# Trailing the feed-forward blocks by four slots instead of two, gathering by column halves, and moving two copies from VectorE to GpSimd

## The chip, the cores and the metric

The kernel runs on one core of one Trainium2 chip. The metric is device time in microseconds (us) of one execution; lower is better. The engines are TensorE (PE, with its weight loads PEld), VectorE (DVE), ScalarE (ACT), GpSimd (POOL) and SyncE (SP, which only issues transfers here).

## The reference

Eight batches of eight heads of causal sliding-window attention with a linear position bias (576 rows, head size 64, window 128), whose output, rows by heads, goes through two matrix products with an ELU between them.

```
scores = scale * np.matmul(q, k.transpose(0, 1, 3, 2))
bias = slopes[:, None, None] * (-np.abs(rel))[None, :, :]
mask = (rel >= 0) & (rel < 128)
attn = softmax(np.where(mask, scores + bias[None], -1e9))
x = np.matmul(attn, v).transpose(0, 2, 1, 3).reshape(B * S, H * D)    # 4608 x 512
h = x @ w_in                                                          # 512 x 2048
g = np.where(h > 0.0, h, np.exp(np.minimum(h, 0.0)) - 1.0)
out = g @ w_out                                                       # 2048 x 512
```

## The kernel before

The whole program is one list of slots, written out by hand. In each slot every engine gets its instructions in the order of the source, and it works them off in that order; there is no scheduler behind it.

**Attention.** Batch b has the sixteen slots from `s0 = 16 b` on. Slot s of it is one call of `scores` (a bank of 512 scores: four matmuls or eight half ones), with the exponential on ScalarE behind it. From batch 1 on the mask is applied by `cut`, a minimum on VectorE over two SBUF operands. One slot later comes `values` (the product with v), in some slots `normalize` (a reciprocal and a product on VectorE), and one slot after that `turn`, which lays 128 rows of the normalised output as columns into `xT`. For batches 0 and 1 `turn` is four PE transposes and a VectorE copy, from batch 2 on a transposing transfer on SP's queue (L424).

**Feed-forward (MoE in the names).** The 4608 rows are cut into nine blocks of 512, each with sixteen calls of `hidden` and sixteen of `output`, one of each per slot. `hidden` is 8 or 16 matmuls into a PSUM bank `hp` (two buffers), then an exponential on ScalarE into `e`, then a clamp of `e` on GpSimd (L457). `elu` on VectorE (L464), one slot later, joins `e` and `hp` into `g` and so frees the `hp` bank. `output` is four matmuls of 512 columns (L493); every fourth one is copied out by ScalarE and stored by SP. The tables `HID` and `OUT` name the slots. Block t begins with `hidden` in slot 4 + 16 t, and from block 2 on two slots later, because its rows are ready only then; so slots 36 and 37 have no `hidden`, and slots 45 and 46 no `output`. In a slot PE does `hidden`, then `values` of the slot before, then `scores`, then `output`. VectorE does `elu` of the slot before first.

**q, k and v of later batches.** GpSimd's queue loads them from HBM (`load_qk`, `load_tail`, `load_v4`, `load_v4_tail`); issuing such a load takes time on GpSimd itself. For batches 2 to 7 q and k are turned to head-size-by-rows form in two steps: `squares` (eight VectorE stream transposes of 32 x 32 squares into the one buffer `tt`, L318) and `collect` (eight SBUF-to-SBUF transfers on SP's queue from `tt` into `QK`, L324). `QK[b % 2]` and `VP[b % 2]` hold q, k and v of a batch. Each of the four row blocks i of `QK` is waited for by its own first `scores`. v is laid into `VP` by four small copies per row block n: `place_v4` does so on VectorE (batches 0 to 2), `place_by_pool` on GpSimd (batches 3 to 7). The constant rows 64 to 127 of `QK[1]`, among them what `fill_k` writes, are made in slots 10 to 14 and copied to `QK[0]` once by a transfer in slot 20 (`fill_other`).

Of the kernel before, what the change touches and what calls it, by code (L numbers as in the profile page):

```python
# [12 lines left out]
ALU = mybir.AluOpType  # L13
# [6 lines left out]
def kernel(  # L20
# [9 lines left out]
    nc = tc.nc  # L30
    B, H, S, D = q.shape
# [4 lines left out]
    NTB = NTOK // 512  # L36
    MID = S // 2
    XBAR = 2
    RING = 3 * S
    VW = D + 2  # L40
    V = nc.vector

# [10 lines left out]
    def one(shape, dt, name):  # L53
        return const.tile(shape, dt, name=name, tag=name)
# [12 lines left out]
    QK = [one([128, 2, 5, H, 128], F16, f"QK{i}") for i in range(2)]  # L67
    VP = [one([128, 5, H, VW], F16, f"VP{i}") for i in range(2)]
    EX = [one([128, 576], F16, f"EX{i}") for i in range(4)]
    w_in_sb = one([128, 4, FF], F16, "wi")  # L70
    w_out_sb = one([128, NFC, DO], F16, "wo")
    xT = one([128, 4, RING], F16, "xT")

# [63 lines left out]
    with tc.manual_schedule():  # L137
# [76 lines left out]
        g_, r_ = slice(64, 96), slice(96, 128)  # L214
# [3 lines left out]
        TK = one([128, 640], F16, "TK")  # L218
# [37 lines left out]
                           TQ[64:128, 128 * n:128 * n + 128].unsqueeze(1).broadcast_to([64, H, 128]))  # L256

        def fill_k(n):
            V.tensor_copy(QK[1][g_, 1, n, :, :],
                          TK[g_, 128 * n:128 * n + 128].unsqueeze(1).broadcast_to([32, H, 128]))  # L260

        def k_term(h):
            V.tensor_scalar(out=QK[1][r_, 1, :, h, :], in0=TK[r_, :].rearrange("p (n c) -> p n c", c=128),
# [49 lines left out]
        def squares(b, n):  # L313

            if b not in tt:
                tt[b] = stage.tile([128, 2, 2, H, 4, 32], F16, name="tt", tag="tt", bufs=1)
            w, dh, hs = 1 - n // 4, n // 2 % 2, slice(4 * (n % 2), 4 * (n % 2) + 4)
            V.transpose(out=tt[b][:, w, dh, hs, :, :].rearrange("p h j i -> p (h j) i"),  # L318
                        in_=stq[b][:, w, hs, :, 32 * dh:32 * dh + 32].rearrange("p h j d -> p (h j) d"))

        def collect(b, n):

            i, dh = n // 2, n % 2
            nc.sync.dma_start(  # L324
                QK[b % 2][32 * dh:32 * dh + 32, :, i, :, :].rearrange("p w h c -> p w (h c)"),
                tt[b][32 * i:32 * i + 32, :, dh, :, :, :].rearrange("p w h j i -> p w (h j i)"))
# [92 lines left out]
        def turn(b, i):  # L419
            n = 128 if i < 4 else 64  # L420
            if b >= XBAR:
                x = xnt.pop((b, i)).rearrange("p h d -> p (h d)")
                o = (b * S + 128 * i) % RING
                nc.sync.dma_start_transpose(out=xT[:, :, o:o + n], in_=x[0:n, :])  # L424
# [3 lines left out]
            for c in range(4):  # L428
                nc.tensor.transpose(t[:, c, :], x[:, c, :], ident)
            o = (b * S + 128 * i) % RING  # L430
            V.tensor_copy(xT[:, :, o:o + n], t[:, :, 0:n])
# [11 lines left out]
        def hidden(t, j):  # L443
            w, c0, f0, nf = place(t, j)
            p = hps[t, j] = ps_h.tile([128, 512], F32, name="hp", tag="hp")
            a = (512 * t + c0) % RING
            cuts = [(0, w, a)] if a + w <= RING else [(0, RING - a, a), (RING - a, w, 0)]
            for l in range(nf):
                fc = f0 + l
                for u0, u1, x0 in cuts:  # L450
                    for c in range(4):
                        nc.tensor.matmul(  # L452
                            p[:, l * w + u0:l * w + u1], w_in_sb[:, c, fc * 128:(fc + 1) * 128],
                            xT[:, c, x0:x0 + u1 - u0], start=(c == 0), stop=(c == 3))
            e = es[t, j] = work.tile([128, 512], F32, name="e", tag="e")
            nc.scalar.activation(e, p, AF.Exp)  # L456
            nc.gpsimd.tensor_scalar(out=e, in0=e, scalar1=1.0, scalar2=0.0, op0=ALU.min, op1=ALU.max)  # L457

        def elu(t, j):
            w, c0, f0, nf = place(t, j)  # L460
            if t not in gs:
                gs[t] = gpool.tile([128, NFC, 512], F16, name="g")
            sh = lambda ap: ap.rearrange("p (l c) -> p l c", c=w)
            V.scalar_tensor_tensor(  # L464
                out=gs[t][:, f0:f0 + nf, c0:c0 + w], in0=sh(es.pop((t, j))), scalar=1.0,
                in1=sh(hps.pop((t, j))), op0=ALU.subtract, op1=ALU.max)
# [36 lines left out]
        def warm(n):  # L503

            for _ in range(n):
                nc.tensor.matmul(spare[:, 0:128], ident, ident, start=True, stop=True)  # L506
# [4 lines left out]
        def at(s, f, *a):  # L511
            tasks.setdefault(s, []).append((f, a))


        HID = {4 + m + (2 if m >= 32 else 0): divmod(m, 16) for m in range(16 * NTB)}
        OUT, O0 = {}, 13
        for t in range(NTB):
            for j in range(16):
                OUT[O0 + 16 * t + j + (2 if t > 1 else 0)] = (t, j)
        warm(34)  # L520
        transposes_half(0, 0)
        transposes_half(0, 1)
# [5 lines left out]
        for b in range(B):  # L528
            s0 = 16 * b
            for s in range(16):  # L530
                i, p = BANKS[s]
                half = p if i in (0, 4) else p // 2
                at(s0 + s, scores, b, s)
                if b:
                    at(s0 + s, cut, b, s)
                at(s0 + s + 1, values, b, s)
                if i in (0, 4) or p % 2:
                    at(s0 + s + 1, normalize, b, i, half)
                    if half:
                        at(s0 + s + 2, turn, b, i)  # L540
            if b == 0:
                at(5, transposes_half, 1, 0)
                at(6, transposes_half, 1, 1)
                at(12, transposes_tail, 0)
            if b + 1 < B:
                for hp in range(NP if b == 0 else 0):
                    at((14, 14, 15, 15)[hp], transposes, 1, hp)
                for n in range(8 if b else 0):
                    at(s0 + (n if b > 1 else 6 + n // 2), squares, b + 1, n)
                    at(s0 + (8 if b > 1 else 10) + n // 2, collect, b + 1, n)  # L550
                at(s0 + (14 if b else 25), transposes_tail, b + 1)
            if b + 2 < B and b:
                at(s0 + 14, load_v4, b + 2)
                at(s0 + 19, load_v4_tail, b + 2)
                for n in range(4):
                    for u in range(2):
                        at(s0 + 20 + 2 * n + u, place_by_pool, b + 2, n, u)
                for i, w in enumerate((1, 0)):
                    at(s0 + 10 + 2 * i, load_qk, b + 2, w)
                    at(s0 + 11 + 2 * i, load_tail, b + 2, w)  # L560
# [10 lines left out]
        for n in range(5):  # L571
            at(10 + n, fill_q, n)
            at(10 + n, fill_k, n)
# [13 lines left out]
        at(11, load_v4, 1)  # L587
        at(14, load_v4_tail, 1)
        at(18, load_v4, 2)
        at(33, load_v4_tail, 2)  # L590
        for n in range(4):
            at(15 + n, place_v4, 1, n)
            at(32 + n, place_v4, 2, n)

        for s in range(max(OUT) + 1):
            if s in HID:
                hidden(*HID[s])
            if s - 1 in HID:
                elu(*HID[s - 1])
            for f, a in tasks.get(s, []):  # L600
# [33 lines left out]
```

## Time and profile before

| what | value |
|---|---|
| three runs, median (lowest to highest) | 372.12 us (369.16 to 373.36) |
| the profiled execution, its own time | 368.4 us |
| its span, first to last instruction | 366.6 us |
| mean granted clock of TensorE, share of full speed | 0.975 |
| busy share of the span: PE, DVE, ACT, POOL | 92%, 71%, 52%, 51% |

The profiled execution is below the fastest of the three runs. 1.8 us of its time lie outside the span. The rows below are from its trace; L numbers are lines of the kernel before.

### The profile page before, as it was taken

The numbers are of one execution on the slowest core, as the hardware profiler recorded it, in microseconds if no ns is written. First come the engines' busy times: TensorE is split into PE (matmuls) and PEld (weight loads), VectorE is DVE, ScalarE is ACT, GpSimd is POOL, SyncE is SP. The second block draws the span as 40 slices with busy tenths as digits, with TensorE's granted clock in tenths as the row PEclk, the third lists the DMA queues.
The fourth block names the chain that finished last, engine by engine and source line by source line (L and its number), as shares of the span: only waits on it lengthen the run. The fifth ranks groups of instructions, "written<-read, shape, count | busy, mean of one in ns | idle before, by whom it ended". The sixth has DMA issues, their size and how long they took to land.

```text
span 366.6 us, 9293 instructions
## 1 busy us (share of the span) xinstructions
PE 335.6 (92%) x3598; PEld 243.9 (67%) x3598; DVE 261.4 (71%) x604; ACT 189.2 (52%) x330; POOL 186.4 (51%) x291
## 2 busy tenths in 40 slices
PE   7879888999767989995999999999999999999994
PEld 6768765767544767774777677767767777766651
DVE  6479998797797769963888598768977766633430
ACT  3464874555333655562565456555565566443431
POOL 9144524435342882884368927883883223233320
PEclk9996999999996999998999999999999999999999
DMA  8999958969921599369935993699363142212112
GB/s 114 201 205 107 170 57 134 196 104 147 194 35 31 115 161 146 59 146 150 122 60 130 141 171 56 142 158 151 66 143 76 37 60 44 52 36 52 30 45 70
DMA packets 67435, 39.53 MB, mean 108 GB/s; under 512 B 30976, under 2 KB 59648, under 8 KB 67328
## 3 DMA queue, kind: packets, MB, share of 16 engines
q0 software_dynamic: 41904, 18.35, 43.7%
q1 hardware_dynamic: 25488, 20.59, 27.8%
q8 instruction: 28, 0.46, 0.6%
q14 instruction: 15, 0.12, 0.1%
HBM read 36.70 MB, written 9.44 MB: 126 GB/s over the span
## 4 chain that ended last, share of the span: by engine, by line
PE 54%; DVE 15%; POOL 14%; DMA 6%; issue 4%; ACT 3%; SPq 1%; ACTq 0%; POOLq 0%; DVEq 0%
PE hp L452 23%; PE op L493 20%; POOL VP L122 7%; PE sp L349 5%; POOL e L457 5%; DMA QK<-tt 4%; DVE VP L117 4%; DVE g L464 3%; PE av L395 3%; DVE tt L318 2%; DMA stq<-in_q_dram 1%; DVE xn L416 1%; DVE EX L381 1%; ACT EX L373 1%; POOL stq L81 1%
## 5 line engine op out<-in xcount | busy, mean ns | idle before, releaser
L457 POOL TENSOR_SCALAR e<-e 128x512 f32<-128x512 f32 x144 | 88.9, 617 | 159.1 <-ACT e L456 155.8
L452 PE MATMUL hp<-xT,wi 128*128 128x256 f16 (+3 forms) x1536 | 153.2, 249 | 13.7 <-DVE g L464 8.6
L452 PEld LDWEIGHTS <-wi 128*128 128x128 f16 x1536 | 123.7, 99 | 56.4 <-issue 12.4
L456 ACT ACTIVATE e<-hp 128x512 f32<-128x512 f32 x144 | 86.0, 597 | 132.7 <-PE hp L452 124.0
L493 PE MATMUL op<-wo,g 128*128 128x512 f16 x576 | 148.2, 383 | 0.0
L464 DVE SCALAR_TENSOR_TENSOR g<-e,hp 128x512 f16<-128x512 f32 x144 | 96.8, 672 | 34.6 <-POOL e L457 33.8
L373 ACT ACTIVATE EX<-sp 128x512 f16<-128x512 f32 x128 | 75.9, 593 | 18.8 <-PE sp L369 10.2
L381 DVE TENSOR_TENSOR EX<-EX,band 128x512 f16<-128x512 f16 x112 | 53.2, 475 | 35.0 <-ACT EX L373 34.7
L493 PEld LDWEIGHTS <-g 128*128 128x128 f16 x576 | 51.6, 99 | 37.5 <-issue 1.1
L122 POOL TENSOR_SCALAR VP<-vs 32x512 f16<-32x512 f16 x80 | 51.4, 643 | 5.5
L349 PE MATMUL sp<-QK 128*128 128x128 f16 (+3 forms) x576 | 50.6, 216 | 0.4 <-DVE QK L297 0.4
L395 PE MATMUL av<-VP,EX 128*128 128x65 f16 x576 | 39.3, 195 | 8.1 <-DVE EX L381 3.8
L395 PEld LDWEIGHTS <-EX 128*128 128x128 f16 x576 | 31.3, 99 | 14.3 <-DVE EX L381 6.6
L416 DVE TENSOR_TENSOR xn<-av,rden 128x256 f16<-128x256 f32 x80 | 33.9, 424 | 2.8
L318 DVE STREAM_TRANSPOSE tt<-stq 128x512 f16<-128x512 f16 x48 | 33.2, 697 | 1.3 <-DMA QK<-tt 1.3
L349 PEld LDWEIGHTS <-QK 128*128 128x128 f16 (+1 forms) x576 | 31.8, 98 | 1.4 <-DVE QK L297 0.5
L497 ACT COPY ob<-op 128x512 f32<-128x512 f32 x36 | 21.1, 586 | 14.8 <-PE op L493 6.5
L415 DVE RECIPROCAL rden<-av 128x4 f32<-128x4 f32 x80 | 13.9, 174 | 13.9 <-PE av L395 13.4
L117 DVE COPY VP<-vs 32x512 f16<-32x512 f16 x48 | 17.0, 354 | 1.0 <-DMA vs<-in_v_dram 0.3
L506 PE MATMUL spare<-ident 128*128 128x128 f16 x94 | 9.0, 273 | 1.6 <-DVE ident L163 1.6
L506 PEld LDWEIGHTS <-ident 128*128 128x128 f16 x94 | 8.1, 128 | 1.7 <-DVE ident L163 1.6
L297 ACT COPY QK<-tp 64x1024 f16<-64x1024 f16 x6 | 6.0, 1008 | 6.2 <-PE tp L288 4.8
(71 smaller groups left out, 124.1 us busy)
## 6 DMA issues: line engine op xcount, KB each, us to landing
out_dram<-ob SPq DMA_DIRECT2D x128, 64.0 KB, 1.7
QK<-tt SPq DMA_DIRECT2D x48, 128.0 KB, 2.5
stq<-in_k_dram POOLq DMA_DIRECT2D x7, 512.0 KB, 8.4
stq<-in_q_dram POOLq DMA_DIRECT2D x7, 512.0 KB, 8.4
vs<-in_v_dram POOLq DMA_DIRECT2D x7, 512.0 KB, 9.8
wi<-in_moe_w_in_dram POOLq DMA_DIRECT2D x4, 512.0 KB, 11.3
wo<-in_moe_w_out_dram POOLq DMA_DIRECT2D x4, 512.0 KB, 12.8
QK<-QK SPq DMA_DIRECT2D x1, 1280.0 KB, 12.9
```

The costliest lines, as they stand in the source:

```text
L122: nc.gpsimd.tensor_scalar(out=VP[b % 2][32 * j:32 * j + 32, n, :, 0:D], in0=vs[b][32 * n:32 * n + 32, :, j, :], scalar1=1.0, scalar2=0.0, ...
L318: V.transpose(out=tt[b][:, w, dh, hs, :, :].rearrange("p h j i -> p (h j) i"), in_=stq[b][:, w, hs, :, 32 * dh:32 * dh + 32].rearrange("p ...
L349: nc.tensor.matmul(t[:, o:o + n], qk[0:r, 1, kc, h, :], qk[0:r, 0, qc, h, 0:n], start=b > 0 or o == 0, stop=b > 0)
L373: nc.scalar.activation(e[:, 0:512], t, AF.Exp, scale=0.125)
L381: V.tensor_tensor(out=e, in0=e, in1=band[:, c:c + n].unsqueeze(1).broadcast_to([128, 512 // n, n]), op=ALU.min)
L395: nc.tensor.matmul(a[:, l, :], e[:, c:c + 128], vp[:, n, h, 0:D + 1], start=st, stop=sp)
L416: V.tensor_tensor(out=xnt[b, i][:, 4 * half:4 * half + 4, :], in0=a[:, :, 0:D], in1=r.unsqueeze(2).broadcast_to([128, 4, D]), op=ALU.mult)
L452: nc.tensor.matmul(p[:, l * w + u0:l * w + u1], w_in_sb[:, c, fc * 128:(fc + 1) * 128], xT[:, c, x0:x0 + u1 - u0], start=(c == 0), stop=(c ...
L456: nc.scalar.activation(e, p, AF.Exp)
L457: nc.gpsimd.tensor_scalar(out=e, in0=e, scalar1=1.0, scalar2=0.0, op0=ALU.min, op1=ALU.max)
L464: V.scalar_tensor_tensor(out=gs[t][:, f0:f0 + nf, c0:c0 + w], in0=sh(es.pop((t, j))), scalar=1.0, in1=sh(hps.pop((t, j))), op0=ALU.subtrac ...
L493: nc.tensor.matmul(ops[t], gs[t][:, fc, ts * 128:(ts + 1) * 128], w_out_sb[:, fc, :], start=(fc == 0), stop=(fc == NFC - 1))
```

## The change

It edits five places.

1. `HID` and `OUT`: from block 2 on, `hidden` and `output` come four slots later than for blocks 0 and 1, not two. So slots 36 to 39 have no `hidden`, slots 45 to 48 no `output`, and the program has two slots more behind the attention.
2. `squares` goes through its eight pieces by halves of the head size (`dh`) first, and for batches 3 to 7 begins two slots later (third slot of the batch before, not first).
3. `collect` goes through the four row blocks of one half, then those of the other. One goes out per slot, in slots 8 to 15 (batch 2) or 6 to 13 (batches 3 to 7) of the batch before, where two per slot went out in slots 10 to 13 or 8 to 11.
4. v of batch 2 is placed by GpSimd (16 instructions, slots 24 to 31) and not by VectorE (16 instructions, slots 32 to 35); its tail is loaded in slot 22, not 33.
5. `fill_k` (five instructions, slots 10 to 14) is on GpSimd, not VectorE.

```diff
+    LATER = 4
         def fill_k(n):
-            V.tensor_copy(QK[1][g_, 1, n, :, :],
-                          TK[g_, 128 * n:128 * n + 128].unsqueeze(1).broadcast_to([32, H, 128]))
+            nc.gpsimd.tensor_scalar(
+                out=QK[1][g_, 1, n, :, :], in0=TK[g_, 128 * n:128 * n + 128].unsqueeze(1)
+                .broadcast_to([32, H, 128]), scalar1=1.0, scalar2=0.0, op0=ALU.mult, op1=ALU.add)
...
-            w, dh, hs = 1 - n // 4, n // 2 % 2, slice(4 * (n % 2), 4 * (n % 2) + 4)
+            dh, w, hs = n // 4, 1 - n // 2 % 2, slice(4 * (n % 2), 4 * (n % 2) + 4)
...
-            i, dh = n // 2, n % 2
+            dh, i = divmod(n, 4)
...
-        HID = {4 + m + (2 if m >= 32 else 0): divmod(m, 16) for m in range(16 * NTB)}
+        HID = {4 + m + (LATER if m >= 32 else 0): divmod(m, 16) for m in range(16 * NTB)}
...
-                OUT[O0 + 16 * t + j + (2 if t > 1 else 0)] = (t, j)
+                OUT[O0 + 16 * t + j + (LATER if t > 1 else 0)] = (t, j)
...
-                    at(s0 + (n if b > 1 else 6 + n // 2), squares, b + 1, n)
-                    at(s0 + (8 if b > 1 else 10) + n // 2, collect, b + 1, n)
+                    at(s0 + (2 + n if b > 1 else 6 + n // 2), squares, b + 1, n)
+                    at(s0 + (6 if b > 1 else 8) + n, collect, b + 1, n)
...
-        at(33, load_v4_tail, 2)
+        at(22, load_v4_tail, 2)
         for n in range(4):
             at(15 + n, place_v4, 1, n)
-            at(32 + n, place_v4, 2, n)
+            for u in range(2):
+                at(24 + 2 * n + u, place_by_pool, 2, n, u)
```

Line numbers after the edit are two higher in most functions. VectorE's instructions from the `cut` of slot 32 on stand so before (EX: exponentials, xn: normalised rows, VP_88: v of even batches):

```order
L381 TENSOR_TENSOR EX_90<-EX_90,band 128x512
L318 STREAM_TRANSPOSE tt<-stq 128x512
L117 COPY VP_88<-vs 32x8x64 x4
L464 SCALAR_TENSOR_TENSOR g<-e,hp 128x4x128
L431 COPY xT<-xps 128x4x64
L415 RECIPROCAL rden<-av 128x4
L416 TENSOR_TENSOR xn<-av,rden 128x256
L381 TENSOR_TENSOR EX_91<-EX_91,band 128x512
```

and so now, from the `cut` of the same slot on:

```order
L383 TENSOR_TENSOR EX_90<-EX_90,band 128x512
L466 SCALAR_TENSOR_TENSOR g<-e,hp 128x4x128
L433 COPY xT<-xps 128x4x64
L417 RECIPROCAL rden<-av 128x4
L418 TENSOR_TENSOR xn<-av,rden 128x256
L383 TENSOR_TENSOR EX_91<-EX_91,band 128x512
```

The stream transpose and the four copies of each slot are gone from between two cuts; the transposes begin behind the cut of slot 34, the copies are no longer on VectorE.

GpSimd's instructions from the load of k of batch 3 in slot 26 on, before (e: the clamps, one per slot; stq, stt: loads of batch 3):

```order
L81 DMA stq_1515<-in_k_dram 128x8x256
L457 TENSOR_SCALAR e_1538<-e_1538 128x512
L102 DMA stt_1562<-in_k_dram 64x8x64
L457 TENSOR_SCALAR e_1585<-e_1585 128x512
L81 DMA stq_1515<-in_q_dram 128x8x256
L457 TENSOR_SCALAR e_1634<-e_1634 128x512
L102 DMA stt_1562<-in_q_dram 64x8x64
```

and now, from the clamp of slot 26 on (VP0: v of even batches, here of batch 2):

```order
L459 TENSOR_SCALAR e_1502<-e_1502 128x512
L82 DMA stq_1521<-in_k_dram 128x8x256
L123 TENSOR_SCALAR VP0_88<-vs_1150 32x8x64 x2
L459 TENSOR_SCALAR e_1546<-e_1546 128x512
L103 DMA stt_1569<-in_k_dram 64x8x64
L123 TENSOR_SCALAR VP0_88<-vs_1150 32x8x64 x2
L459 TENSOR_SCALAR e_1594<-e_1594 128x512
L82 DMA stq_1521<-in_q_dram 128x8x256
L123 TENSOR_SCALAR VP0_88<-vs_1150 32x8x64 x2
```

Two placing instructions stand now in each slot from 24 to 31, ahead of the next clamp, and in five of these slots (26 to 30) the issue of a load stands ahead of them.

SP's queue in slots 55 to 60, where the third row block of batch 3 is turned (second transpose here), before:

```order
L424 DMA_TRANSPOSE xT<-xn 128x4x128
L324 DMA QK_86<-tt 32x2x1024 x6
L499 DMA out_dram<-ob 32x512 x4
L424 DMA_TRANSPOSE xT<-xn 128x4x128
L324 DMA QK_86<-tt 32x2x1024 x2
```

and now:

```order
L426 DMA_TRANSPOSE xT<-xn 128x4x128
L326 DMA QK_86<-tt 32x2x1024 x2
L501 DMA out_dram<-ob 32x512 x4
L326 DMA QK_86<-tt 32x2x1024 x2
L426 DMA_TRANSPOSE xT<-xn 128x4x128
```

The transpose stood behind six gathers and a store of four pieces since the transpose ahead of it, and now behind four gathers and the store.

## Rows read from the trace of the kernel before

**Rows 1.** Page, busy time and share of the span by engine.
```profile
PE 335.6 (92%) x3598; PEld 243.9 (67%) x3598; DVE 261.4 (71%) x604; ACT 189.2 (52%) x330; POOL 186.4 (51%) x291
```
**Rows 2.** Stretches of 8 us: busy time by engine, PEclk granted clock, DMA.
```profile
104.00:112.00 8.00, 4.58 (x40) 2.39 (x40) 7.76 (x18) 2.11 (x4) 4.09 (x7) 0.85 0.21 25
112.00:120.00 8.00, 6.59 (x52) 4.30 (x52) 5.32 (x12) 2.64 (x6) 1.90 (x4) 0.73 0.23 51
...
168.00:176.00 8.00, 4.54 (x39) 3.33 (x40) 3.05 (x9) 1.69 (x3) 3.07 (x5) 0.79 1.44 143
...
184.00:192.00 8.00, 8.00 (x80) 5.88 (x78) 7.09 (x16) 4.63 (x9) 5.31 (x9) 1.00 0.34 58
```
**Rows 3.** PE timeline, slots 24 to 40: start, length, work, [idle before <- releaser].
```profile
76.02 0.39 PE L349 MATMUL sp<-QK 128*128 128x128 f16 x4
...
95.49 0.39 PE L349 MATMUL sp<-QK 128*128 128x128 f16 x4
...
100.35 0.30 PE L395 MATMUL av<-VP,EX 128*128 128x65 f16 x4 [2.50 <-DVE VP L117]
...
109.24 0.29 PE L395 MATMUL av<-VP,EX 128*128 128x65 f16 x4 [1.96 <-DVE EX L381]
...
121.21 0.39 PE L349 MATMUL sp<-QK 128*128 128x128 f16 x4
```
**Rows 4.** VectorE timeline: v copies of batch 1, stream transpose and copies in slots 32 to 35.
```profile
52.95 1.17 DVE L117 COPY VP<-vs 32x512 f16<-32x512 f16 x4
...
98.31 0.71 DVE L318 STREAM_TRANSPOSE tt<-stq 128x512 f16<-128x512 f16 x1 [1.29 <-DMA QK<-tt]
...
109.82 1.94 DVE L117 COPY VP<-vs 32x512 f16<-32x512 f16 x4
```
**Rows 5.** Timelines of POOL, DVE and PE over one slot without a stall.
```profile
84.61 0.61 POOL L457 TENSOR_SCALAR e<-e 128x512 f32<-128x512 f32 x1 [1.57 <-ACT e L456]
...
85.51 0.68 DVE L464 SCALAR_TENSOR_TENSOR g<-e,hp 128x512 f16<-128x512 f32 x1
...
86.16 0.39 PE L349 MATMUL sp<-QK 128*128 128x128 f16 x4
...
87.24 1.06 PE L452 MATMUL hp<-xT,wi 128*128 128x128 f16 x16
...
87.36 0.46 DVE L381 TENSOR_TENSOR EX<-EX,band 128x512 f16<-128x512 f16 x1 [0.36 <-ACT EX L373]
...
88.26 0.39 PE L349 MATMUL sp<-QK 128*128 128x128 f16 x4
```
**Rows 6.** Timeline at slot 62, and landing times of all transposing transfers (L424).
```profile
163.69 2.07 SPq L424 DMA_TRANSPOSE xT<-xn  x1
...
171.46 1.86 PE L452 MATMUL hp<-xT,wi 128*128 128x256 f16 x8 [3.77 <-issue]
...
DMA to landing us min/median/max: 2.3/3.2/9.3
```
**Rows 7.** Timeline of slots 42 to 47, POOL and PE.
```profile
126.36 0.61 POOL L457 TENSOR_SCALAR e<-e 128x512 f32<-128x512 f32 x1
...
127.06 1.34 POOL L122 TENSOR_SCALAR VP<-vs 32x512 f16<-32x512 f16 x2
...
128.46 0.93 POOL L81 DMA_DIRECT2D stq<-in_k_dram  x1
...
133.69 1.05 PE L452 MATMUL hp<-xT,wi 128*128 128x256 f16 x8 [1.39 <-DVE g L464]
...
134.69 0.40 PE L349 MATMUL sp<-QK 128*128 128x64 f16 x8
...
136.66 0.40 PE L349 MATMUL sp<-QK 128*128 128x64 f16 x8
```
**Rows 8.** Groups by line, VectorE, 30 to 56 us: fill_k.
```profile
L259 DVE COPY QK<-TK 32x1024 f16<-32x1024 f16 x5 | 2.3, 454 | 0.1
```
**Rows 9.** Chain that ended last, a piece in the slots behind the attention.
```profile
347.17 0.87 PE hp L452 x8
```

## The prediction

> **What bounds the kernel now.** I began with busy time by engine. PE is busy 335.6 of 366.6 us [rows 1], and the change neither adds nor removes a matmul, so only PE's idle time (31 us) and its time at half clock can move. The stretches of 8 us then show where these lie. From about 248 us on PE is busy without a gap, and in an earlier steady stretch (184 to 192 us, slots 67 to 70) too [rows 2], although by the slot tables VectorE does squares there and GpSimd places v. The two bad stretches in the change's reach are 104 to 120 us, with 4.58 and 6.59 us of PE work in 8 and a granted clock of 0.85 and 0.73, and 168 to 176 us, with 4.54 us and 0.79 [rows 2]. The clock is at one of two levels, 2.4 or 1.2 GHz, so 0.79 over 8 us means (1 - 0.79) x 2 x 8 = 3.4 us at the lower. In both places PE had stood idle just before.
>
> Next I read PE's timeline for the names of the waits. From the scores of slot 32 to those of slot 40 PE needs 121.21 - 95.49 = 25.7 us [rows 3]. It waits 2.50 us for v copies of VectorE, then 1.96 us (and a like wait a slot later) for a masked EX, which is also VectorE [rows 3]. VectorE's own timeline says why: each of slots 32 to 35 has a stream transpose and four v copies queued between two cuts, the first transpose after 1.29 us of waiting for the gathers out of `tt`, and the copies take up to 1.94 us a slot [rows 4]. The other place is slot 62: `hidden` of block 3's second half stands 3.77 us without a named releaser [rows 6]. It reads columns whose transposing transfer was issued at 163.69 us, in slot 59, so it started 7.8 us after that issue. Transfers of that line land after 3.2 us as a median and 9.3 at most [rows 6], so I read this as a late landing.
>
> A slot without a stall takes 88.26 - 86.16 = 2.10 us [rows 5]. A block of `hidden` or of `output` is about 0.87 us of it [rows 9].
>
> **The change part by part.**
>
> *Slots 32 to 39 (lead of four, squares two slots later, v off VectorE).* Slots 33, 34 and 35 and the step into slot 40 should be full ones: 4 x 2.10 = 8.4 us. VectorE then has no v copies; squares come from slot 34. Slots 36 to 39 have no `hidden`, and there PE's work (about 1.2 us) is shorter than the attention's own chain. That chain, from scores to the end of the cut, is 87.36 + 0.46 - 86.16 = 1.66 us [rows 5], and with the v product ahead of the next scores about 1.8. GpSimd places batch 3's v there, which can lengthen the cut, so I take 2.0: four times is 8.0 us. Together 16.4 against 25.7, that is 9.3 us less. Two `hidden` blocks have moved behind the attention, where they cost 0.87 each [rows 9]: **+7.6 us**. Bounds: 8.3 at 1.8 a slot; 4.6 if the clock falls in these four slots as it did in 104 to 120 us, which I put at 3 us. The wait of the first transpose for `tt` goes: it overwrites the first half of the head size, whose four gathers are out by slot 27, seven slots ahead.
>
> *Slots 45 to 48 (no `output`), two before, four now.* Such a slot took 136.66 - 134.69 = 1.97 us [rows 7], with a small transpose of the rows' tail in it. Leaving out `output` hence saves 0.13 to 0.3 of a 2.10 us slot, while its 0.87 us comes back at the end: 0.57 to 0.74 lost a slot, two slots: **-1.3 us** (-1.1 to -1.5).
>
> *Slot 62, now 64.* The lead gives the transfer two more slots, 4.2 us, more than the 3.77 missing; it also stands behind fewer gathers since the transpose ahead of it. Its margin is then five slots, 10.5 us, above the longest landing of 9.3. With the wait goes the half clock behind it: eight matmuls took 1.86 us [rows 6] for 1.05 [rows 7], 0.8 us, and at most half of 3.4 us, 1.7; I take 1.2. **+5.0 us**; bounds 0 (a landing later still) and 5.5.
>
> *GpSimd in slots 24 to 31.* Clamp and two placements repeat every 128.46 - 126.36 = 2.10 us [rows 7]: as much as a full slot, with nothing to spare. Five of these slots now also issue a load, 0.93 us for a large one [rows 7], and I take that for the small ones too. 8 x 2.10 + 5 x 0.93 = 21.5 us, for a stretch in which PE takes 95.49 - 76.02 = 19.5 us [rows 3]. Slack: a clamp that ended at 84.61 + 0.61 = 85.22 let `elu` end at 85.51 + 0.68 = 86.19, for a bank that `hidden` took at 87.24 [rows 5], so 1.05 us. Over the stretch that leaves 1.0 us of stall; over slots 26 to 30 alone, at 2.10 each for PE, 5 x 0.93 - 1.05 = 3.6. The nearest row, the same meeting of placements and loads in slots 42 to 44, stopped PE 1.39 us [rows 7], with two loads among the placements. **-2.0 us**, bounds 0 and -3.6. The order of work doesn't let VectorE go around it: `elu` stands ahead of the cut in each slot, so a late clamp holds up the attention too.
>
> *fill_k.* VectorE loses 5 x 0.454 = 2.3 us [rows 8] where it has almost no idle time (0.1 us before all five). GpSimd gets five instructions of twice the elements per partition of a placement (1.34 for two [rows 7]), so about 1.3 us each, between clamps. Clamps of slots 12 to 14 come later by up to a microsecond, but VectorE is itself late for them. **+0.6 us**; bounds -1 and +2.3.
>
> *At nothing:* the tail load of v moved to slot 22 (GpSimd stood idle 1.57 us before a clamp nearby [rows 5]; uncovered, 0.9 us). Squares and gathers later: row block 0 of the next batch now needs the gathers of the first and the fifth place, six slots (12.6 us) ahead of its scores in batches 3 to 7 and four (at least 8.4 us) in batch 2. Against the nearest landing row, 9.3 at most [rows 6], that could cost batch 2 0.9 us. On SP a gather waits for its squares, and stores and transposes queue behind it; those squares stand two slots or more ahead, so I see no new hold.
>
> *What speaks against it.* Four v copies took 1.17 us when GpSimd placed nothing, and 1.94 when it did [rows 4]: 0.8 us more for four. The Trainium skill, page "SBUF — State Buffer", section "Who interferes with whom", says that a VectorE instruction with two SBUF inputs, or in a two-port mode, and a GpSimd instruction that reads SBUF shut each other out for a whole instruction. The rows agree that they lengthen each other, and the rule adds that each cut, with its two SBUF operands, could wait a whole placement. By it slots 24 to 31 would come out as in the first rival below.
>
> **Sum.** 7.6 - 1.3 + 5.0 - 2.0 + 0.6 = 9.9 us. The profiled execution took 368.4 us, so 358.5 for its like. It lies 3.7 us below the median, and the times shown are medians: 372.1 - 9.9 = **362.2 us**.
>
> **The rivals.**
>
> 1. *GpSimd becomes the bound in slots 24 to 31 (and 10 to 14).* The lag takes its full 3.6 us, and each of eight cuts waits for part of a placement: one placement is 0.67 us, eight are 5.4, of which I let half show, 2.7, and fill_k gains nothing. 9.9 + 2.0 - 3.6 - 2.7 - 0.6 = 5.0 gained: 367.1 us. For it: no spare time in rows 7. Against it: lag is made good in slots 32 to 39.
> 2. *The late landing stays.* Slot 64 waits as slot 62 did because the transfer shares the queue with gathers that now run on to the end of the batch: 9.9 - 5.0 = 4.9, so 367.2 us. Against it: two slots of lead are more than the wait.
> 3. *The clock falls in the thin slots.* Slots 36 to 39 and 45 to 48 leave PE about 60 to 65% busy; 57% went with 0.85 [rows 2]. 3 us lost: 365.2 us.
> 4. *Slower.* Squares and placements now share six slots of a batch, not four. If there VectorE waits a whole placement for each of the two in a slot, 1.34 us over two slots in five batches is 13.4 us, 375.7 us. It decides once PE's gaps there pass 1 us a slot on average (9.9 / 10). Against it: 184 to 192 us, where both already meet, has no gap on PE [rows 2].
> 5. *It doesn't do what it says:* the lead gives room, but other waits of the same slots come in its place, and 2 us are left: 370.1 us.
>
> **How the numbers follow.** My forecast, 358 to 365 us, gets 0.58; the rivals get 0.15, 0.08, 0.07, 0.06 and 0.06. The bounds of the terms reach from 0.5 to about 15 us gained, 357 to 371.6. From 357 to 368.5 the range holds the forecast, rivals 2 and 3 and most of rival 1. About 1% (3.7 us) is what a measurement of this kernel tells from no change, so faster means below 368.4: forecast 0.58, 0.12 of rival 1, 0.07 and 0.07 of rivals 2 and 3, 0.84 in all; slower 0.05; the rest, 0.11, within 1%.
>
> **What would show it.** Right: from the scores of slot 32 to those of slot 40 about 16 us, no waits on v copies there, PE idle about 0.6 us a slot in 36 to 39; no gap before the first `hidden` of slot 64; PE waits for `elu` and VectorE for GpSimd's clamp around slots 29 to 33, 2 us in all. Wrong: a gap of over 3 us at slot 64; clamps late by several us around slot 31; a clock below 1.00 in slots 36 to 48; new PE gaps in batches 3 to 7 where squares and placements meet.

## The result, and the profile after

The changed kernel takes 359.28 us (median of four runs, 358.97 to 359.77), and the kernel before, in four runs beside it, 370.64 us (368.45 to 373.36). The ratio is 0.969, with a 95% interval of 0.962 to 0.977: **faster**. The forecast was 362.2 us in a range of 357.0 to 368.5. In the two traces the saving is smaller, since the profiled execution of before is the fastest of its runs: 368.4 against 358.97 us, spans 366.6 against 357.2 us, 9.4 us less. The sum of the prediction, 9.9 us, was made against that execution. Two runs are left out of the ratios as slow, one of the lead of one below (677.03 us, which nothing here explains) and one of the kernel before beside it (376.67 us).

The busy times on the page of the changed kernel answer to [rows 1]:

```profile
PE 331.0 (93%) x3598; PEld 240.2 (67%) x3598; DVE 254.3 (71%) x583; ACT 189.5 (53%) x330; POOL 202.4 (57%) x312
```

GpSimd has 16 us more, VectorE 7 us less, and PE 4.6 us less for the same matmuls, at a mean granted clock of 0.989 instead of 0.975. Stretches of 8 us, with the columns of [rows 2]:

```profile
104.00:112.00 8.00, 5.40 (x49) 2.72 (x49) 6.58 (x13) 2.98 (x6) 6.03 (x10) 1.00 0.40 69
112.00:120.00 8.00, 8.00 (x81) 5.88 (x79) 6.60 (x14) 4.45 (x8) 5.46 (x9) 1.00 0.48 106
160.00:168.00 8.00, 8.00 (x116) 6.29 (x115) 6.35 (x17) 4.14 (x8) 3.84 (x6) 1.00 1.49 168
...
184.00:192.00 8.00, 7.92 (x76) 5.29 (x75) 5.89 (x13) 4.56 (x10) 7.20 (x12) 1.00 0.50 101
```

The first stretch holds the four slots without `hidden`. PE is idle for 2.6 of 8 us, and the granted clock is 1.00 all the same, where [rows 2] had 0.85 and 0.73. The third holds slots 62 to 65, with no gap.

PE's timeline from slot 32 to slot 40 answers to [rows 3]:

```profile
95.73 0.39 PE L351 MATMUL sp<-QK 128*128 128x128 f16 x4
...
97.38 1.07 PE L454 MATMUL hp<-xT,wi 128*128 128x128 f16 x16 [0.39 <-DVE g L466]
...
104.67 0.39 PE L351 MATMUL sp<-QK 128*128 128x128 f16 x4
...
106.62 0.30 PE L397 MATMUL av<-VP,EX 128*128 128x65 f16 x4 [0.70 <-DVE EX L383]
106.75 0.39 PE L351 MATMUL sp<-QK 128*128 128x128 f16 x4
108.74 0.29 PE L397 MATMUL av<-VP,EX 128*128 128x65 f16 x4 [0.73 <-DVE EX L383]
108.87 0.39 PE L351 MATMUL sp<-QK 128*128 128x128 f16 x4
...
113.05 0.39 PE L351 MATMUL sp<-QK 128*128 128x128 f16 x4
```

From slot 32 to slot 40 it takes 113.05 - 95.73 = 17.32 us, against 25.72 us [rows 3]. The waits for v copies and the 1.96 us wait for EX are gone. Left are waits of about 0.7 us for EX in slots 37 to 39, which therefore take 2.1 us each, like a full slot. Why, GpSimd's and VectorE's timelines of these slots show:

```profile
104.91 5.60 POOL L123 TENSOR_SCALAR VP<-vs 32x512 f16<-32x512 f16 x8
...
104.41 0.70 DVE L320 STREAM_TRANSPOSE tt<-stq 128x512 f16<-128x512 f16 x1
105.04 0.64 DVE L466 SCALAR_TENSOR_TENSOR g<-e,hp 128x512 f16<-128x512 f32 x1
...
105.81 0.42 DVE L418 TENSOR_TENSOR xn<-av,rden 128x256 f16<-128x256 f32 x1
106.15 0.41 DVE L383 TENSOR_TENSOR EX<-EX,band 128x512 f16<-128x512 f16 x1
...
107.81 0.87 DVE L383 TENSOR_TENSOR EX<-EX,band 128x512 f16<-128x512 f16 x1 [0.62 <-ACT EX L375]
...
109.92 0.86 DVE L383 TENSOR_TENSOR EX<-EX,band 128x512 f16<-128x512 f16 x1
```

The first of the three waits ends behind a cut of the usual 0.41 us, which came late because a square, `elu` and `normalize` stood ahead of it in VectorE's queue. For the other two, GpSimd's eight placements of 0.70 us run without a pause beside the cuts, and two cuts take twice the usual time.

GpSimd and VectorE in slots 29 to 33, from the stretch of the -2.0 us to just behind it:

```profile
88.48 1.51 POOL L123 TENSOR_SCALAR VP<-vs 32x512 f16<-32x512 f16 x2
90.07 0.61 POOL L459 TENSOR_SCALAR e<-e 128x512 f32<-128x512 f32 x1
...
90.72 0.69 DVE L466 SCALAR_TENSOR_TENSOR g<-e,hp 128x512 f16<-128x512 f32 x1 [1.21 <-POOL e L459]
...
96.63 0.69 DVE L466 SCALAR_TENSOR_TENSOR g<-e,hp 128x512 f16<-128x512 f32 x1 [1.21 <-POOL e L459]
```

VectorE waits 1.21 us for late clamps, twice. On PE, slots 24 to 32 take 20.62 us (75.11 to 95.73) instead of the 19.47 us of [rows 3].

Last, the transposing transfer of slot 59, the store behind it, the load of k beside it, the first `hidden` that reads it, and the landings of all such transfers (L426). The first fence is the changed kernel. The second is the one row of before that [rows 6] lacks, the load of k, issued 0.71 us *ahead* of the transfer there (the transfer landed 7.7 us after its own issue):

```profile
152.92 1.22 SPq L426 DMA_TRANSPOSE xT<-xn  x1
...
157.50 1.75 SPq L501 DMA_DIRECT2D out_dram<-ob  x4
...
154.49 0.94 POOL L82 DMA_DIRECT2D stq<-in_k_dram  x1
...
164.52 1.04 PE L454 MATMUL hp<-xT,wi 128*128 128x256 f16 x8
...
DMA to landing us min/median/max: 2.3/2.6/10.8
```

```profile
162.98 0.93 POOL L81 DMA_DIRECT2D stq<-in_k_dram  x1
```

The transfer now goes out 1.57 us ahead of the load and lands after 2.5 us, and `hidden` has no wait. Transfers at other places still land as late as 10.8 us, with nobody waiting.

### The profile page after: what moved, and what is told of

It is laid out like the page before. It is cut to its first block, busy times and chain, and to the rows that moved or that the text cites. A ratio compares the mean times of both kernels' runs of the same rounds, so it can differ in the third digit from the quotient of the medians.

```text
span 357.2 us, 9287 instructions
## 1 busy us (share of the span) xinstructions
PE 331.0 (93%) x3598; PEld 240.2 (67%) x3598; DVE 254.3 (71%) x583; ACT 189.5 (53%) x330; POOL 202.4 (57%) x312
## 4 chain that ended last, share of the span: by engine, by line
PE 60%; POOL 13%; DVE 10%; ACT 6%; issue 5%; DMA 3%; SPq 1%; ACTq 0%; POOLq 0%
PE hp L454 26%; PE op L495 23%; POOL VP L123 7%; PE sp L351 5%; POOL e L459 4%; PE av L397 3%; DVE g L466 3%; ACT EX L375 2%; DVE VP L118 2%; DVE tt L320 2%; ACT e L458 2%; DVE EX L383 2%; DMA stq<-in_q_dram 1%; ACT QK L256 1%; SPq L501 1%
## 5 line engine op out<-in xcount | busy, mean ns | idle before, releaser
L454 PE MATMUL hp<-xT,wi 128*128 128x256 f16 (+3 forms) x1536 | 151.2, 247 | 11.4 <-DVE g L466 9.7
L454 PEld LDWEIGHTS <-wi 128*128 128x128 f16 x1536 | 122.1, 98 | 53.2 <-DVE g L466 11.8
L495 PE MATMUL op<-wo,g 128*128 128x512 f16 x576 | 146.4, 379 | 0.0
L383 DVE TENSOR_TENSOR EX<-EX,band 128x512 f16<-128x512 f16 x112 | 54.2, 484 | 32.1 <-ACT EX L375 31.6
L123 POOL TENSOR_SCALAR VP<-vs 32x512 f16<-32x512 f16 x96 | 62.0, 646 | 6.5
L351 PE MATMUL sp<-QK 128*128 128x128 f16 (+3 forms) x576 | 49.8, 213 | 0.4 <-DVE QK L299 0.4
L397 PEld LDWEIGHTS <-EX 128*128 128x128 f16 x576 | 30.5, 98 | 11.8 <-DVE EX L383 6.8
L118 DVE COPY VP<-vs 32x512 f16<-32x512 f16 x32 | 11.0, 344 | 0.5
```

The lines of the kernel that those rows point to most:

```text
L123: nc.gpsimd.tensor_scalar(out=VP[b % 2][32 * j:32 * j + 32, n, :, 0:D], in0=vs[b][32 * n:32 * n + 32, :, j, :], scalar1=1.0, scalar2=0.0, ...
L351: nc.tensor.matmul(t[:, o:o + n], qk[0:r, 1, kc, h, :], qk[0:r, 0, qc, h, 0:n], start=b > 0 or o == 0, stop=b > 0)
L383: V.tensor_tensor(out=e, in0=e, in1=band[:, c:c + n].unsqueeze(1).broadcast_to([128, 512 // n, n]), op=ALU.min)
L397: nc.tensor.matmul(a[:, l, :], e[:, c:c + 128], vp[:, n, h, 0:D + 1], start=st, stop=sp)
L454: nc.tensor.matmul(p[:, l * w + u0:l * w + u1], w_in_sb[:, c, fc * 128:(fc + 1) * 128], xT[:, c, x0:x0 + u1 - u0], start=(c == 0), stop=(c ...
L495: nc.tensor.matmul(ops[t], gs[t][:, fc, ts * 128:(ts + 1) * 128], w_out_sb[:, fc, :], start=(fc == 0), stop=(fc == NFC - 1))
```

## The experiments

All times are medians of four runs; ratios are against the kernel before on the same chip. Spans are those of the profiled executions; before 366.6, changed kernel 357.2 us.

### Which part of the lead does the work at slot 62

**Lead of two**, the rest as changed.

```diff
-    LATER = 4
+    LATER = 2
```

> The changed kernel with a lead of two slots again, all else kept. A, as I predicted (the lead is what met the late landing): the wait of about 4 us is back before the first hidden of slot 62, and two thin slots of each kind fewer save 2 x 0.87 + 2 x 0.68 = 3.1 us, so 359.3 - 3.1 + 4.5 = 360.7 us. B, read from the trace after (the transfer of slot 59 went out at 152.92 us, ahead of that slot's scores at 153.50, and landed in 2.5 us, where before it took 7.7 us): the new order of the gathers cured it and the lead only costs, so no wait at slot 62 and 359.3 - 3.1 = 356.2 us.

361.50 us, ratio 0.974 (0.968 to 0.981). Timelines of GpSimd, SP and PE, the landing of that one transfer, then two stretches of 2 us inside the wait:

```profile
153.26 0.93 POOL L82 DMA_DIRECT2D stq<-in_k_dram  x1
...
152.14 1.74 SPq L501 DMA_DIRECT2D out_dram<-ob  x4
...
153.98 1.96 SPq L426 DMA_TRANSPOSE xT<-xn  x1
...
163.18 1.87 PE L454 MATMUL hp<-xT,wi 128*128 128x256 f16 x8 [5.22 <-DMA xT<-xn]
...
DMA to landing us min/median/max: 9.1/9.1/9.1
```

```profile
158.00:160.00 2.00, 0.00 (x0) 0.00 (x0) 1.45 (x3) 0.00 (x0) 1.86 (x3) 1.00 6.94 136
160.00:162.00 2.00, 0.00 (x0) 0.00 (x0) 0.00 (x0) 0.00 (x0) 0.00 (x0) 1.00 0.31 26
```

The wait is back, as theory A had it, and the half clock behind it (eight matmuls in 1.87 us, as in [rows 6], and not 1.04). But the rows show more than a lead too short: the transfer is issued 0.72 us *behind* the load of k, because with a lead of two a store of `output` stands ahead of it on SP's queue (four issues, 1.74 us), and it lands after 9.1 us instead of 2.5. In the second stretch DMA moves only 26 GB/s while the transfer is still out, so it isn't plain bandwidth that it waits for there. The packets in the trace say more: some seventy of both queues that begin between 158.8 and 159.7 us stay open for 2.2 to 3.0 us (the DMA share of 6.94, where 1 is all 16 engines, adds them up) and end together at 161.8, 1.3 us ahead of the landing. Nearly all transfers stand at that time, not this one alone.

**Lead of one**, the rest as changed (`LATER = 1`).

> The changed kernel with a lead of one slot. A: waits before the first hidden of several half blocks, 363 us or more. B: each slot of lead costs 0.87 + 0.68 = 1.55 us, so 359.3 - 4.6 = 354.7 us, if the first hidden of slot 37 (its transfer goes out in slot 35 and lands in 2.5 us) and of slot 53 (its last transfer landed at 139.2 us in the trace after, slot 53 begins near 140) do not wait; up to 1.5 us of wait at slot 53 is in it, 356.2 us.

357.62 us, ratio 0.960 (0.953 to 0.967): faster than with two, where theory A had 363 or more and theory B 354.7 to 356.2. The load of k goes out later here (155.50), the transfer 0.68 us ahead of it (154.82), and it lands after 5.0 us. PE waits 1.97 us at slot 61 and 0.40 us at slot 45 for such transfers: a shorter lead, and a shorter wait. So the lead by itself doesn't decide it.

**The lead alone**, on the kernel before.

```diff
-        HID = {4 + m + (2 if m >= 32 else 0): divmod(m, 16) for m in range(16 * NTB)}
+        HID = {4 + m + (4 if m >= 32 else 0): divmod(m, 16) for m in range(16 * NTB)}
...
-                OUT[O0 + 16 * t + j + (2 if t > 1 else 0)] = (t, j)
+                OUT[O0 + 16 * t + j + (4 if t > 1 else 0)] = (t, j)
```

> The kernel before with a lead of four slots and nothing else. A and B agree that the wait of slot 62 goes (a landing of 7.7 us against a missing 3.8 us and 4.2 us of lead): 4.5 us less. The v copies stay in slots 32 to 35, where VectorE is the bound. Price of the lead 3.1 us, so 370.6 - 4.5 + 3.1 = 369.2 us; less if the thin slots 36 to 39 hide part of the v copies, down to 367.

366.07 us, ratio 0.985 (0.980 to 0.991); span 364.3 us, 2.3 less than before, and 0.9 us below the range expected (367 to 369.2). No wait at slot 64: the transfer is issued at 161.04, the load of k at 161.78, and it lands after 2.5 us, with the old gathers. The waits for VectorE's copies stay: slots 32 to 40 take 25.4 us.

**Squares and gathers alone**, on the kernel before.

```diff
-            w, dh, hs = 1 - n // 4, n // 2 % 2, slice(4 * (n % 2), 4 * (n % 2) + 4)
+            dh, w, hs = n // 4, 1 - n // 2 % 2, slice(4 * (n % 2), 4 * (n % 2) + 4)
...
-            i, dh = n // 2, n % 2
+            dh, i = divmod(n, 4)
...
-                    at(s0 + (n if b > 1 else 6 + n // 2), squares, b + 1, n)
-                    at(s0 + (8 if b > 1 else 10) + n // 2, collect, b + 1, n)
+                    at(s0 + (2 + n if b > 1 else 6 + n // 2), squares, b + 1, n)
+                    at(s0 + (6 if b > 1 else 8) + n, collect, b + 1, n)
```

> The kernel before with the new order and slots of squares and gathers and nothing else (lead two, v of batch 2 and fill_k on VectorE). A: the wait at slot 62 stays within a microsecond; only the waits of slots 32 and 33 shrink (the 1.29 us for the gathers and two stream transposes of 0.7 us that leave these slots), 370.6 - 2.7 = 367.9 us. B: the wait at slot 62 goes as well, 367.9 - 4.5 = 363.4 us.

367.61 us, ratio 0.989 (0.984 to 0.994), and a span of 366.5 us, 0.1 less than before. Slots 32 to 40 take 23.1 us, 2.6 less, and slot 62 gives it back: the transfer is issued at 160.85, 0.72 us behind the load of k, lands after 9.3 us, and PE waits 5.43 us. Fewer gathers ahead of the transfer do nothing for its landing. GpSimd, SP and PE:

```profile
160.13 0.93 POOL L81 DMA_DIRECT2D stq<-in_k_dram  x1
...
160.85 3.13 SPq L424 DMA_TRANSPOSE xT<-xn  x1
...
170.26 1.87 PE L452 MATMUL hp<-xT,wi 128*128 128x256 f16 x8 [5.43 <-DMA xT<-xn]
```

**`hidden` back to a lead of two, `output` at four**, the rest as changed.

```diff
-        HID = {4 + m + (LATER if m >= 32 else 0): divmod(m, 16) for m in range(16 * NTB)}
+        HID = {4 + m + (2 if m >= 32 else 0): divmod(m, 16) for m in range(16 * NTB)}
```

> The changed kernel with hidden trailing by two slots but output still by four. Theory A: it is the place of the output stores on SyncE's queue that decides: with output at four the store is not ahead of the transposing transfer of slot 59, which goes out before the load of k and lands in about 2.5 us; no wait at slot 62 although hidden leads by two: 357.5 to 359 us. Theory B: hidden's lead decides: a wait of 3 us or more at slot 62, about 361 us or above.

357.40 us, ratio 0.965 (0.959 to 0.970); span 355.2 us. SP, GpSimd and PE at slots 59 to 62, and the landing:

```profile
152.85 1.22 SPq L426 DMA_TRANSPOSE xT<-xn  x1
...
154.41 0.93 POOL L82 DMA_DIRECT2D stq<-in_k_dram  x1
...
159.63 1.05 PE L454 MATMUL hp<-xT,wi 128*128 128x256 f16 x8 [0.53 <-DVE g L466]
...
DMA to landing us min/median/max: 2.5/2.5/2.5
```

Theory A held. Between this run and the lead of two only the slots of `output` differ, and the wait of 5.22 us is gone. With `hidden` at two, slots 38 and 39 take 2.08 us each, no more than without `hidden` (2.12 and 2.10), and two blocks less come behind the attention: 2 x 0.87 = 1.74 of the 2.0 us that the span is shorter.

**Loads of k two slots later and of q three, lead of two.** v's load keeps its slot and now stands between k and q.

```diff
-    LATER = 4
+    LATER = 2
...
-                    at(s0 + 10 + 2 * i, load_qk, b + 2, w)
-                    at(s0 + 11 + 2 * i, load_tail, b + 2, w)
+                    at(s0 + 12 + 3 * i, load_qk, b + 2, w)
+                    at(s0 + 13 + 3 * i, load_tail, b + 2, w)
```

> The changed kernel with a lead of two, as in the first experiment, but the loads of k and q begin two slots later in each batch (slot 12, not 10). Theory A: the transposing transfer of slot 59 lands late only because it is issued behind GpSimd's large load of k and shares the DMA engines with it; issued ahead of it, it lands in about 2.5 us, and two slots of lead suffice: no wait at slot 62, and the 1.4 us wait at slot 45, where loads and placements met, is gone too: 353.5 to 356 us. Theory B: the lead itself gives the room: the wait of 5.2 us at slot 62 stays, about 361 us.

351.74 us, ratio 0.949 (0.944 to 0.954), better than either theory's figure; span 351.2 us. SP, GpSimd, PE, and the landing:

```profile
152.46 1.73 SPq L501 DMA_DIRECT2D out_dram<-ob  x4
...
154.29 2.06 SPq L426 DMA_TRANSPOSE xT<-xn  x1
...
156.33 0.94 POOL L82 DMA_DIRECT2D stq<-in_k_dram  x1
...
157.95 1.04 PE L454 MATMUL hp<-xT,wi 128*128 128x256 f16 x8
...
DMA to landing us min/median/max: 3.3/3.3/3.3
```

The store stands ahead of the transfer, as in the first experiment, and no wait follows, because the load now comes behind both. The 1.40 us wait for `g` (the expectation says slot 45; by the order of work in a slot it is slot 46's `hidden`) is gone too, and so are waits of 0.53 us in slots 62, 78 and 94: there loads and placements had met in GpSimd's queue. A new wait of 0.78 us stands in slot 70; the joined kernel below doesn't have it.

### The placing of v, and fill_k

**v of batch 2 on VectorE again.**

```diff
-        at(22, load_v4_tail, 2)
+        at(33, load_v4_tail, 2)
...
-            for u in range(2):
-                at(24 + 2 * n + u, place_by_pool, 2, n, u)
+            at(32 + n, place_v4, 2, n)
```

> The changed kernel with v of batch 2 placed by VectorE in slots 32 to 35 again. Theory A: the placing is worth a term of its own; without it slots 32 to 40 take about 22.5 us again and not 17.3, and the 1.15 us of lag in slots 24 to 32 is not there: 359.3 + 5.2 - 1.15, about 363.3 us, with PE waiting for v copies in slots 33 to 36. Theory B: lead of four and gathers by halves did it, and the copies fit beside them: 359.3 us or 1 us below, no waits on v copies.

362.62 us, ratio 0.979 (0.975 to 0.982); span 360.9 us. Theory A held. VectorE and PE:

```profile
105.65 2.71 DVE L118 COPY VP<-vs 32x512 f16<-32x512 f16 x4
...
110.01 0.40 PE L397 MATMUL av<-VP,EX 128*128 128x65 f16 x4 [3.56 <-DVE EX L383]
```

Slots 32 to 40 take 22.1 us, 4.8 more, and slots 24 to 32 take 19.5, 1.1 less. The wait is for EX because the cut stands behind the copies in VectorE's queue.

**v of batch 2 six slots sooner**, ahead of the loads of batch 3.

```diff
-        at(18, load_v4, 2)
-        at(22, load_v4_tail, 2)
+        at(14, load_v4, 2)
+        at(17, load_v4_tail, 2)
...
-                at(24 + 2 * n + u, place_by_pool, 2, n, u)
+                at(18 + 2 * n + u, place_by_pool, 2, n, u)
```

> The changed kernel with v of batch 2 loaded four slots earlier and placed in slots 18 to 25, ahead of most loads of batch 3. Theory A: GpSimd's lag of slots 24 to 32 (1.15 us to 1.9 us on PE) comes from placements and loads in the same slots; apart, it goes: 357.4 to 358.1 us. Theory B: placing costs its lag wherever it stands, since clamp and two placements fill a slot of 2.1 us: 359.3 us or above, waits for clamps in slots 18 to 25 in place of those in 24 to 31.

357.52 us, ratio 0.966 (0.961 to 0.972); span 355.5 us. Theory A held: VectorE waits for no clamp in slots 24 to 34, slots 24 to 36 take 28.25 us instead of 29.56, 1.31 less, and slots 14 to 24 are the same within 0.1 us (30.22 and 30.15). The lag was the meeting of placements and loads, not the placing.

**Batch 3's first eight placements on ScalarE.**

```diff
+    def place_by_act(b, n, u):
+        for j in (2 * u, 2 * u + 1):
+            nc.scalar.copy(VP[b % 2][32 * j:32 * j + 32, n, :, 0:D], vs[b][32 * n:32 * n + 32, :, j, :])
...
+                        if b > 1 or n > 1:
+                            at(s0 + 20 + 2 * n + u, place_by_pool, b + 2, n, u)
...
+                if n < 2:
+                    at(36 + 2 * n + u, place_by_act, 3, n, u)
```

> The changed kernel with the first eight placements of batch 3's v, slots 36 to 39, on ScalarE and not GpSimd. Theory A: the cuts of the four thin slots take 0.86 us and not 0.43 because GpSimd places v beside them; without that they take 0.43 to 0.46, the slots 1.8 us and not 2.1, together 1.2 us: 358.1 us. Theory B: the cut is long there for another reason, or ScalarE's own copies hold up the exponentials: cuts 0.86 or exponentials later, slots 2.1, 359.3 us or above.

358.05 us, ratio 0.967 (0.963 to 0.971). It lies where theory A put it, but not for its reason. ScalarE and VectorE in slots 36 to 38:

```profile
104.57 1.25 ACT L129 COPY VP<-vs 32x512 f16<-32x512 f16 x2
105.84 0.59 ACT L503 COPY ob<-op 128x512 f32<-128x512 f32 x1
106.32 0.60 ACT L379 ACTIVATE EX<-sp 128x512 f16<-128x512 f32 x1
...
106.95 0.42 DVE L387 TENSOR_TENSOR EX<-EX,band 128x512 f16<-128x512 f16 x1 [0.98 <-ACT EX L379]
```

The cuts take 0.41 to 0.42 us, so GpSimd's placements had made them long. But the next exponential now stands behind ScalarE's copies, the cuts wait for it, and slots 36 to 40 take 8.08 us instead of 8.38: 0.3 us gained, not 1.2, and most of it is lost again by slot 45. The rest of the difference arose before slot 14, where this kernel and the changed one are the same program.

**fill_k on VectorE again** (the reverse of its part of the diff).

> The changed kernel with fill_k on VectorE again. Theory A: the 0.9 to 1.1 us gained before slot 24 come from fill_k: 360.2 to 360.4 us, PE's scores of slot 16 about 0.9 us later. Theory B: they come from the start of the run or the clock there, not from fill_k: 359.3 us, slot 16 as before.

360.32 us, ratio 0.973 (0.970 to 0.977), 1.04 us slower, which is theory A's size, though the two intervals overlap. What the rows add: PE again waits 0.36 us for `xT` in slot 12 and for `g` in slot 14, as in before:

```profile
45.84 1.05 PE L453 MATMUL hp<-xT,wi 128*128 128x128 f16 x16 [0.68 <-DVE g L465]
```

Over all traces, from slot 10's scores to slot 16's PE needs 18.75 to 18.80 us where fill_k is on VectorE (four traces) and 17.84 to 17.92 us where it is on GpSimd (ten): 0.9 us, shown. Where slot 10 starts differs by up to 2.3 us between traces, so one pair of totals could not have told it.

### Joined

**Later loads, lead of two, v of batch 2 sooner**: the edits of two experiments above together.

> Lead of two, loads of k and q two slots later, v of batch 2 placed in slots 18 to 25. If the two terms add: the value of the run with the later loads less 1.3 us, about 352.5 to 354.5 us. If they meet elsewhere (loads of batch 3 then stand in slots 28 to 32 either way, and the lag goes with one of the two changes alone): no faster than that run.

350.59 us, ratio 0.946 (0.941 to 0.950), 1.15 us less than without v sooner, near the 1.3 expected. The intervals of the two overlap, but the rows agree: slots 24 to 36 take 28.24 us instead of 29.87. Its busy times, from the page:

```profile
PE 330.5 (95%) x3598; PEld 241.9 (69%) x3598; DVE 255.7 (73%) x583; ACT 189.1 (54%) x330; POOL 201.4 (58%) x312
```

Behind slot 27, PE has gaps of 0.45 and 0.69 us in slots 36 and 37 and one of 0.15 us in slot 46, and no more.

**The same with a lead of one.**

> As the run before, with a lead of one. If a lead of one leaves room for the transfers once they land in 2.5 us: one more block is not put off behind the attention, 0.5 to 0.9 us faster than with a lead of two, about 352 to 354 us. If not: a wait of 0.4 us or more at slots 45 and 61 that takes this back.

350.15 us, ratio 0.945 (0.940 to 0.950). The 0.4 us between the two is less than either run's spread, and the spans stand the other way (349.6 and 348.8 us): waits of 0.78 and 0.45 us for EX in slots 45 and 46 and of 0.50 us for a transfer in slot 61 take back the block that is saved. Of the 0.8 us between the spans, 0.7 arose in slots 25 and 26, where the two are still the same program. Set against the changed kernel by their ratios to before, both are about 2.4% below it.

## Why the prediction was right, and where it was not

Each term, measured between the two traces by the start of the scores of the slots around it:

| term | predicted (bounds) | measured | from |
|---|---|---|---|
| slots 32 to 39 | +7.6 (4.6 to 8.3) | +6.7 | 25.72 - 17.32, less 2 x 0.87 |
| slots 45 to 48 | -1.3 (-1.1 to -1.5) | -1.4 | 0.36 gained at slot 49, less 2 x 0.87 |
| slot 62, now 64 | +5.0 (0 to 5.5) | +4.5 | lead over before 8.5 us at slot 61, 13.0 at slot 64 |
| GpSimd, slots 24 to 31 | -2.0 (-3.6 to 0) | -1.15 | 20.62 - 19.47 |
| fill_k | +0.6 (-1 to +2.3) | +0.9 | 18.75 - 17.89, slots 10 to 16 |
| sum | +9.9 | +9.6 | spans: +9.4 |

**Slots 32 to 39.** The mechanism was right, and the size was off by 0.9 us. The four steps without `hidden` were put at 8.0 us and took 8.13 (1.83, 2.08, 2.12 and 2.10). The four full steps were put at 8.4 and took 9.19, nearly all of the excess in the step to slot 33 (2.90). There `hidden` started 0.55 us late behind a late clamp, and batch 1's last PE transposes, which the sum left out, took 0.22. The first part is GpSimd's lag reaching further, so the lag is 1.15 + 0.55 = 1.7 us in all, near the 2.0 foreseen. That it goes when placements and loads are kept apart was shown. Of the 8.4 us that these slots became shorter, moving v is worth 4.8 with the rest in place, the squares and gathers 2.6 by themselves, and the lead 0.3 by itself. With a lead of two the slots take 17.26 us with two blocks of `hidden` more in them, so the lead's 1.74 us bought nothing here.

**The thin slots.** Cuts of 0.87 and 0.86 us beside GpSimd's placements, and of 0.41 to 0.42 with the placements moved to ScalarE, show that a placement can hold up a cut; the one at 106.15 us, beside placements too, took 0.41. The Trainium skill, page "SBUF — State Buffer", section "Who interferes with whom", has this as an exclusive lock for a whole instruction, between a VectorE instruction with two SBUF inputs and a GpSimd instruction that reads SBUF. The traces agree for two of these three cuts, and the cost seen is up to 0.46 us a cut, less than a whole placement of 0.70. How long a thin slot would be with neither cost was not measured: ScalarE's copies brought a wait of their own.

**Slot 62.** The size was right, the reason only half. "Fewer gathers" fell: alone they left a wait of 5.43 us. "The lead gives the transfer two more slots" is true by arithmetic (issued at 152.92 and landing 9.1 us later, it would still have been in time for 164.52), but it isn't what the change brought: the transfer landed in 2.5 us. What happened is that the lead moved the store that stood directly in front of the transfer on SP's queue to behind it (157.50), and the transfer so went out ahead of GpSimd's load of k. Moving `output` alone, or the loads alone, did the same with `hidden` at two. In all fourteen traces the landing of slot 59's transfer follows that order. Issued 0.7 us behind the load of k it took 7.7, 9.1 and 9.3 us (before, lead of two, gathers alone). Issued ahead of it, it took 2.5 us in the seven traces where the issue itself lasted 1.2 us, and 3.3 to 5.0 us in the four where it lasted 1.6 to 2.1 us. The store in front doesn't by itself make a landing late: with the loads later it stood there too, and the landing took 3.3 us. The prediction read the landing as given and bought time for it, at 1.7 us for two blocks of `hidden`.

**Why the load holds the transfer** is open. The stretch at 26 GB/s speaks against plain bandwidth. The gathers alone had one too (41 GB/s from 166 to 168 us), and in all three late traces packets of both queues stay open for up to 2.1 to 3.0 us and end together, at 161.8, 168.6 and 170.5 us, 0.9 to 1.6 us ahead of the landing; in the other eleven no such group stands at this transfer. What stops them isn't shown, and it makes up only a part of the delay of 5 to 7 us. The Trainium skill, page "DMA: Bandwidth & Descriptors", section "Queues, rings and completion order", says that each DMA engine takes turns between its queues packet by packet. No run here shows which DMA engine a packet is on, and a hold of 9.1 us, as long as the load's own landing, is more than such a turn would suggest.

**fill_k, slots 45 to 48** came out as worked out, though GpSimd's part of fill_k took 1.04 us an instruction, not 1.3. Dropping `output` from a slot saves PE almost nothing, since the attention's chain or a wait for `g` fills the room.

**The rivals.** GpSimd was late but not the bound, though four of the eight cuts in slots 24 to 31 did take 0.52 to 0.82 us; the lag was not made good in slots 32 to 39 but grew there; the late landing did not stay; the clock stayed at 1.00 in all stretches from 32 to 349 us, with PE idle a third of 104 to 112 us; and squares beside placements cost nothing that shows (in batch 5's, slots 68 to 73, PE has no gap; the stretch 184 to 192 us lies mostly behind them now). The forecast of 362.2 us was 2.9 us high mostly because the saving was taken off a median of 372.1 us, which with the fourth run is 370.6, and the medians differ by 2 us more than the profiled executions do. Two sums of the prediction are off: its bounds add up to -1.5 to 15, not 0.5 to 15 (372.1 + 1.5 = 373.6 us at the upper end), and rival 4 to 375.6 us; the stated range rests on neither.

## What to carry to other kernels

When a transfer lands late, look at what was issued just ahead of it on *every* queue, and move that or the transfer, before giving its reader more time. Where each slot must cover several engines' work, keep bulk loads and copies of the same engine in different slots: a queue with no spare time passes each extra issue on to whoever waits for it. And an engine's work left out of a slot saves only what the slot's next longest chain leaves, here almost nothing.

## What was not expected of the hardware

A transposing transfer of 128 x 512 values landed in 2.5 us or in 9.3 us when it was issued 0.7 us ahead of or behind a 512 KB load on another engine's queue. During such a hold, DMA moved only 26 GB/s for 2 us in one trace and 41 in another, with packets of both queues open for up to 3 us. ScalarE's copy of 32 x 512 values took 0.62 us, about as long as its exponential over 128 x 512 (0.60 us) and only a little less than GpSimd's 0.64 to 0.70.
